# Another order of score tiles, value products and transposes in the first batch of a fused attention, gated-FFN and token-mixing kernel

## The chip, the cores and the metric

The kernel runs on one core of a Trainium2 chip. The time is that of the device for one execution, in microseconds (us); lower is better. The engines are named as the profile names them: PE (TensorE, with PEld for its weight loads), DVE (VectorE), ACT (ScalarE), POOL (GpSimd) and SP (SyncE, which here issues every DMA; SPq in the trace).

## What is computed

Three stages follow each other, in float32, for 4 batches of 576 tokens. Causal attention with 8 heads of 64 channels has a decay bias that comes from a running sum of `s`. A gated FFN (512 to 1024 channels) mixes its gate over the tokens. A last stage mixes tokens with two 576x576 matrices. Cut to what matters:

```python
scores = scale * q @ k.T + min(-(cum_i - cum_j), 0)      # cum = cumsum(relu(s)), causal mask
attn = softmax(scores); x = concat_heads(attn @ v)       # [4, 576, 512]
h = gelu(x @ w_in); u, v = h[..., :512], h[..., 512:]
x2 = x + (u * (w_sg @ layernorm(v) * g_ln + b_sg)) @ w_out
theta = x2 @ w_theta
y = w_tok_r @ (x2 * cos(theta)) + w_tok_i @ (x2 * sin(theta))
out = (x2 + y) + relu((x2 + y) @ w_ch)
```

## The kernel before

**Precision.** Products are made of halves: each operand is rounded (`rnd`, L82 on ACT, L86 on POOL) and its rest is kept (`sub`, L90), so that most products are three matmuls. The FFN's weights arrive as 64-bit words and are converted by `split64`: an ACT scaling of the raw words (L465, `wtab<-wraw`), three DVE integer operations (L466, L467, L469), an ACT rounding (`wih`, L82) and a POOL rest (`wil`, L90). The weights `w_sg` come through `gt` into `wsh` and `wsl`.

**Heads.** `attention` runs through the 32 heads. For head g it draws on three generators. `score_units(g)` has six units: four score tiles `sc` of 128, 192, 320 and 448 columns, and one wide tile `sc2` (2 x 288 columns) in two units. Each tile gets a row maximum on DVE (L292) and an exponential on ACT (L293), which writes `E`. `transpose_units(g - 1)` transposes the `E` of the head in front on PE (L332) and copies the results to `Ef` and `E0`. It also sends the reciprocal row sums through `R`, `rT` and the DRAM buffer `rd`. After every second head `pv_units` makes the value product `Y` of a pair of heads, and a small remainder `Z` that is written into a corner of the wide score tile then in use. DVE multiplies both with the factors `xT`, loaded back from `rd` (L390 for `Z`, L391 for `Y`). `split_head(g + 2)` and `load_head(g + 4)` prepare later heads: a POOL rounding of `qA`, POOL rests for `qA` and `kB`, and loads of `Q` and `K`.

**Buffers.** The four `sc` tiles, `R`, `Y` and (from the second batch on) the transposes share four PSUM buffers. The wide tile has one buffer, so that the next wide tile waits for the exponential of this one and for L390, which reads `Z` out of it. In the first batch the transposes have two PSUM buffers of their own. The parts `qB` and `kB` have two buffers, one for even and one for odd heads.

**What sets the order.** `ORDER` and `ORDER_V` (L56, L57) are strings that are followed for every head: `s` draws a score unit, `t` a transpose unit, `v` a value unit, and `p` prepares later heads (and loads `xT`). After a batch of 8 heads its FFN becomes a filler: `pace` draws small pieces of it between the units of the following heads. In the first batch there is no such filler. What the code says is then sorted by a list scheduler, which simulates the engines and sets the final order of each engine's instructions; each engine works through its own list strictly in that order. A batch's first FFN products (`fo`) need the converted `w_in`, whose loads (`wraw`) are held back until the loads of head 10.

Of the kernel before, what the change touches and what calls it, by code (L numbers as in the profile page):

```python
# [18 lines left out]
B, H, S, D = 4, 8, 576, 64  # L19
# [30 lines left out]
class Kernel:  # L50
# [2 lines left out]
    LATER, LATER_W = 10, 0  # L53


    ORDER = "ssstsstspttt"  # L56
    ORDER_V = "sssvtsvstspvttt"  # L57
    RATIO_IN, RATIO_GATE, RATIO_W = 0.94, 0.66, 0.8

    def __init__(self, tc, q, k, v, s, w_in, g_ln, w_sg, b_sg, w_out, w_th, w_tr, w_ti, w_ch, out):  # L60
# [358 lines left out]
    def attention(self):  # L419
        n = B * H  # L420
        self.load_head(2)
        self.load_v(2)
        self.load_head(3)
        for g in range(n + 1):
            su = self.score_units(g) if g < n else iter(())
            tu = self.transpose_units(g - 1) if g > 0 else iter(())

            gp = g - 2 if (g - 2) % H != H - 1 else 0
            pv = self.pv_units(gp) if gp > 0 and gp % 2 else iter(())
            if g == n:  # L430
                self.wide = None
            for o in self.ORDER_V if gp > 0 and gp % 2 else self.ORDER:
                if o == "p":
                    if g > 0 and g % 2 == 0:
                        self.load_r(g // 2 - 1)
                    if g + 2 < n:
                        self.split_head(g + 2)
                    if g + 4 < n:
                        self.load_head(g + 4)
                    if g % 2 and g + 3 < n:  # L440
                        self.load_v(g + 3)
                    continue
                c = next({"s": su, "t": tu, "v": pv}[o], None)
                if c is not None:
                    self.pace(c)
            self.run_units([tu])
            if g > 0 and g % H == 0:
                self.run_units([self.pv_units(g - 1)])
                b = g // H - 1
                if b < B - 1:  # L450
                    self.drain()
                    self.fill = self.ffn(b)
# [524 lines left out]
```

## Time and profile before

| | us |
|---|---|
| median of 3 runs | 708.98 (708.6 to 710.29) |
| the profiled execution | 710.52 |
| its span, first to last instruction | 708.7 |
| what lies around the span | 1.8 |
| PE busy in the span | 662.4 (93%) |
| heads 0 to 7 up to the end of pair 3's value product | the first 76.3 |

The profile shows one execution. A row of the timeline has the start, the duration, the engine, the line and the operation; in brackets at its end stands the idle time before it and what ended that. Many PE instructions have L93, since one helper records them; the tile's name tells them apart.

### The profile page before, as it was taken

Reading aid. Unit: us, or ns where it says so; the run is one execution under the profiler, and the core shown is the slowest. Engines: PE = TensorE matmul, PEld = TensorE weight load, DVE = VectorE, ACT = ScalarE, POOL = GpSimd, SP = SyncE. Lnnn points to the kernel's source line nnn. Section 1 sums busy time; section 2 is a strip of 40 time slices with the busy share of each in tenths; the row PEclk is TensorE's granted clock in tenths of the full one; section 3 lists DMA queues with packets and bytes.
Section 4 is the critical chain, followed back from the end, with each engine's and each line's share of the span. In section 5 each row is a group of like instructions: output and inputs, shape, how many; then the busy total and the mean of one; then the engine's idle time right before and its main releaser. Section 6 shows DMA issues by size and latency. Waiting matters only on the chain.

```text
span 708.7 us, 12076 instructions
## 1 busy us (share of the span) xinstructions
PE 662.4 (93%) x4288; PEld 580.9 (82%) x4288; DVE 455.4 (64%) x902; ACT 371.7 (52%) x856; POOL 261.3 (37%) x273
## 2 busy tenths in 40 slices
PE   6899789799999999999999769998999999999998
PEld 4667557588879788897879669887999989989997
DVE  5566687766438544484449998898976368368522
ACT  3566656677367743786427534673753255156100
POOL 6556564458426554375237653423000100010000
PEclk9899989999999999999999989999999999999999
DMA  4646666624423354321143778972000300300101
GB/s 131 188 142 193 203 196 182 183 78 147 125 83 109 102 154 142 103 84 44 68 143 104 243 240 297 328 255 85 34 1 25 110 1 1 134 1 1 68 1 68
DMA packets 52972, 85.02 MB, mean 120 GB/s; under 512 B 9968, under 2 KB 19600, under 8 KB 52912
## 3 DMA queue, kind: packets, MB, share of 16 engines
q1 hardware_dynamic: 52912, 84.25, 38.3%
q8 instruction: 34, 0.56, 0.3%
q14 instruction: 26, 0.21, 0.1%
HBM read 60.38 MB, written 19.10 MB: 112 GB/s over the span
## 4 chain that ended last, share of the span: by engine, by line
PE 49%; DVE 7%; DMA 4%; ACT 3%; issue 2%; POOL 0%; SPq 0%; DVEq 0%; ACTq 0%
PE yo L93 16%; PE co L93 7%; PE fo L93 7%; PE th L93 6%; PE Y L93 3%; PE wo L93 3%; PE sc L93 3%; PE T L332 2%; DVE wta L469 1%; DVE wta L467 1%; DMA x2T<-x2d 1%; PE tp L720 1%; DVE wta L466 1%; DVE gl L90 1%; DMA wraw<-in_moe_w_ch 1%
## 5 line engine op out<-in xcount | busy, mean ns | idle before, releaser
L293 ACT ACTIVATE E<-sc,negm 128x448 f32<-128x448 f32 (+4 forms) x160 | 87.0, 551 | 51.4 <-DVE negm L292 50.3
L292 DVE TENSOR_REDUCE negm<-sc 128x1 f32<-128x448 f32 (+4 forms) x160 | 73.6, 481 | 43.4 <-PE sc L93 42.2
L93 PE MATMUL yo<-wkh,zl 128*128 128x288 f32 x288 | 85.3, 297 | 0.0
L93 PE MATMUL yo<-wkh,zh 128*128 128x288 f32 x288 | 85.2, 296 | 0.0
L93 PE MATMUL yo<-wkl,zh 128*128 128x288 f32 x288 | 85.1, 296 | 0.0
L332 PE MATMUL T<-ident,E 128*128 128x128 f32 x400 | 73.4, 298 | 5.0 <-ACT E L293 3.4
L93 PE MATMUL sc<-kA,qA 128*128 128x128 f32 (+2 forms) x192 | 64.9, 359 | 9.5 <-ACT E L293 7.8
L332 PEld LDWEIGHTS T<-ident,E 128*128 128x128 f32 x400 | 58.2, 194 | 17.2 <-issue 5.7
L93 PE MATMUL sc<-kB,qB 68*128 68x128 f32 (+3 forms) x192 | 61.6, 331 | 3.4 <-DMA qB<-cpos 1.8
L93 PE MATMUL fo<-x,wih 128*128 128x288 f32 x256 | 58.4, 306 | 1.5 <-ACT vT L607 0.8
L86 POOL TENSOR_SCALAR xt<-x2s 128x128 fp32r<-128x128 f32 x16 | 9.9, 634 | 134.2 <-DVE x2s L90 134.2
L93 PEld LDWEIGHTS yo<-wkh,zh 128*128 128x128 f32 x288 | 54.1, 188 | 0.3
L93 PEld LDWEIGHTS yo<-wkl,zh 128*128 128x128 f32 x288 | 54.1, 188 | 0.2
L93 PEld LDWEIGHTS yo<-wkh,zl 128*128 128x128 f32 x288 | 53.9, 188 | 0.2
L93 PE MATMUL co<-u,wch 128*128 128x288 f32 x256 | 53.1, 295 | 0.0
L93 PEld LDWEIGHTS sc<-kA,qA 128*128 128x128 f32 x192 | 38.6, 209 | 16.3 <-ACT E L293 8.4
L90 POOL TENSOR_TENSOR kB<-K,kA 64x576 fp32r<-64x576 f32 x32 | 46.6, 1456 | 10.5 <-ACT kA L82 9.1
L93 PE MATMUL wo<-gh,woh 128*128 128x288 f32 x128 | 40.4, 319 | 9.1 <-DVE xr L697 6.4
L86 POOL TENSOR_SCALAR qA<-Q 128x576 fp32r<-128x576 f32 x32 | 22.6, 705 | 69.7 <-PE sc L93 29.9
L90 POOL TENSOR_TENSOR qA<-Q,qA 64x576 fp32r<-64x576 f32 x32 | 46.3, 1446 | 2.6
L93 PE MATMUL Y<-Ef,vr 128*64 128x512 f32 (+3 forms) x256 | 47.0, 444 | 0.0
L93 PEld LDWEIGHTS fo<-x,wih 128*128 128x128 f32 x256 | 43.3, 192 | 3.9 <-issue 1.2
(169 smaller groups left out, 1878.5 us busy)
## 6 DMA issues: line engine op xcount, KB each, us to landing
Q<-in_q SPq DMA_DIRECT2D x64, 144.0 KB
K<-in_k SPq DMA_DIRECT2D x64, 144.0 KB
qB<-qA SPq DMA_DIRECT2D x32, 144.0 KB
xT<-rd SPq DMA_DIRECT2D x32, 144.0 KB
xd<-xT SPq DMA_DIRECT2D x16, 288.0 KB
gd<-uT SPq DMA_DIRECT2D x16, 288.0 KB
gr<-gd SPq DMA_DIRECT2D x16, 288.0 KB
xr<-xd SPq DMA_DIRECT2D x16, 288.0 KB
```

What stands on the lines that cost most here:

```text
L86: nc.gpsimd.tensor_scalar(out, src, 1.0, 1.0, op0=ALU.mult, op1=ALU.mult)
L90: e.tensor_tensor(out, a, f32(hi), op=ALU.subtract)
L93: self.nc.tensor.matmul(out, lhsT, rhs, start=start, stop=stop)
L292: nc.vector.tensor_reduce(negm[:, c:c + 1], o, axis=ax, op=ALU.max, negate=True)
L293: nc.scalar.activation(out, o, AF.Exp, bias=negm[:, c:c + 1], accum_out=sm[:, j * 5 + c:j * 5 + c + 1])
L332: nc.tensor.transpose(T[:, col:col + P], e, self.ident)
L466: nc.vector.tensor_scalar(ta.bitcast(U32), ta.bitcast(U32), 3, None, op0=ALU.logical_shift_left)
L467: nc.vector.scalar_tensor_tensor(ta.bitcast(U32), Hi, 0x80000000, ta.bitcast(U32), op0=ALU.bitwise_and, op1=ALU.bitwise_or)
L469: nc.vector.scalar_tensor_tensor(ta.bitcast(U32), L, 29, ta.bitcast(U32), op0=ALU.logical_shift_right, op1=ALU.bitwise_or)
L720: nc.tensor.transpose(tp[0:r, dt * P:(dt + 1) * P], x2T[:, dt, a:a + r], self.ident)
```

## The change

Up to and with head 8 (`g <= H`) two other strings are followed. All six score units of a head stand first, then `p`. Where a pair's value product is due, its three units come next (`ALONE_V`). The transposes of the head in front come last. A new letter `r` separates the loading of `xT` from `p`: in the later batches it stands right ahead of `p`, as before, and in the new order it stands after the second transpose unit, which writes `rd`.

```diff
-    ORDER = "ssstsstspttt"
+    ORDER = "ssstsstsrpttt"
     ORDER_V = "sssvtsvstspvttt"
+
+    ALONE, ALONE_V = "sssssspttrttt", "sssssspvvvttt"
...
-            for o in self.ORDER_V if gp > 0 and gp % 2 else self.ORDER:
-                if o == "p":
+            order = (self.ORDER, self.ORDER_V, self.ALONE, self.ALONE_V)
+            for o in order[2 * (g <= H) + (gp > 0 and gp % 2)]:
+                if o == "r":
                     if g > 0 and g % 2 == 0:
                         self.load_r(g // 2 - 1)
+                    continue
+                if o == "p":
                     if g + 2 < n:
                         self.split_head(g + 2)
```

The lines of the file move by two ahead of `attention` (L93 becomes L95). The scheduler sorts the new text anew, so that the lists of all engines differ from head 1 on, on PE until late in the attention. Three places follow. In their names a number behind a tile tells one buffer from another.

**First place: PE in the middle of the batch, around the value product of pair 2 (heads 4 and 5).** Before, between score tiles of head 7; the fences have the matmuls of this stretch in the order in which PE runs them:

```order
L93 MATMUL sc<-kA,qA 128x192
L93 MATMUL sc<-kA,qA 128x320
L332 MATMUL T<-ident,E 128x128 x3
L93 MATMUL Y<-E_75,v_79 128x512
L93 MATMUL Y<-Ef,vr 64x512 x2
L332 MATMUL T<-ident,E 128x128 x2
L93 MATMUL Y<-Ef,vr 64x384 x2
L93 MATMUL Y<-Ef,vr 64x128 x2
L93 MATMUL Y<-Ef,vr 64x256 x2
L93 MATMUL sc<-kB_74,qB_73 128x128
L93 MATMUL sc<-mask,identr 128x128
```

With the change, the same place (`sc_734` is the wide tile of head 6, `sc_815` that of head 7):

```order
L95 MATMUL sc_734<-kB_72,qB_71 128x288
L95 MATMUL sc_734<-mask,identr 128x128
L95 MATMUL sc<-kA,qA 128x448
L95 MATMUL sc<-kB_74,qB_73 128x448
L95 MATMUL sc<-mask,identr 128x128
L95 MATMUL Y<-E_75,v_79 128x512
L95 MATMUL Y<-Ef,vr 64x512 x2
L95 MATMUL Y<-Ef,vr 64x384 x2
L95 MATMUL Y<-Ef,vr 64x128 x2
L95 MATMUL Y<-Ef,vr 64x256 x2
L95 MATMUL sc_815<-kA,qA 128x288
```

The value product has moved behind all four narrow score tiles of head 7, and nothing stands between its parts any more; the head's wide tile follows it, and the wide tile of the head in front stands just ahead. The six score units do not end up in a row.

**Second place: DVE and SP where the first weights are converted.** `sc_1072` to `sc_1104` are score tiles of head 10, `sc2_1031` is the wide tile of head 9, and L390 to L391 (L392 to L393 with the change) take `Z` and `Y` of pair 3 (heads 6 and 7). DVE before:

```order
L292 TENSOR_REDUCE negm1_86<-sc_1091 128x1
L390 TENSOR_TENSOR xT_932<-sc2_913,xT_932 128x64
L391 TENSOR_TENSOR xT_932<-Y_963,xT_932 128x512
L292 TENSOR_REDUCE negm1_86<-sc_1104 128x1
L292 TENSOR_REDUCE negm0_85<-sc2_1031 128x1
L252 TENSOR_SCALAR Q2_945<-Q2_945 128x576
L312 TENSOR_SCALAR sm1_90<-sm1_90 128x10
```

DVE with the change:

```order
L294 TENSOR_REDUCE negm1_86<-sc_1104 128x1
L254 TENSOR_SCALAR Q2_924<-Q2_924 128x576
L471 TENSOR_SCALAR wtab_991<-wtab_991 128x512
L472 SCALAR_TENSOR_TENSOR wtab_991<-wraw_990,wtab_991 128x512
L474 SCALAR_TENSOR_TENSOR wtab_991<-wraw_990,wtab_991 128x512
L471 TENSOR_SCALAR wtab_991<-wtab_991 128x512
L392 TENSOR_TENSOR xT_948<-sc2_906,xT_948 128x64
L393 TENSOR_TENSOR xT_948<-Y_963,xT_948 128x512
L472 SCALAR_TENSOR_TENSOR wtab_991<-wraw_990,wtab_991 128x512
L474 SCALAR_TENSOR_TENSOR wtab_991<-wraw_990,wtab_991 128x512
L294 TENSOR_REDUCE negm0_85<-sc2_1031 128x1
```

The products with `xT` now stand behind one whole weight conversion and the first step of a second; before, they stood ahead of all conversions. The DMA queue of SP at the same place, before:

```order
L362 DMA xT_932<-rd_61 64x576 x2
L227 DMA Q2_945<-in_q 64x576 x2
L229 DMA K2_946<-in_k 64x576 x2
L402 DMA xd_57<-xT_932 128x576
L462 DMA wraw_990<-in_moe_w_in 128x1024 x2
```

SP with the change:

```order
L231 DMA K2_925<-in_k 64x576 x2
L229 DMA Q2_924<-in_q 64x576 x2
L348 DMA rd_61<-rT_945 10x128
L467 DMA wraw_990<-in_moe_w_in 128x1024 x2
L364 DMA xT_948<-rd_61 64x576 x2
```

The loads of `xT` have moved behind the first two loads of weights.

**Third place: PE behind the wide tile of head 9.** Before:

```order
L93 MATMUL sc2_1031<-mask_161,identr_154 128x128
L332 MATMUL T_1120<-ident_149,E_881 128x128 x2
L332 MATMUL T_1098<-ident_149,E_881 128x128
L93 MATMUL sc2_1117<-kA_936,qA_935 128x288
L93 MATMUL sc2_1117<-kB0_72,qB0_71 128x288
L332 MATMUL T_1120<-ident_149,E_881 128x128 x2
```

With the change:

```order
L95 MATMUL sc2_1031<-mask_161,identr_154 128x128
L95 MATMUL fo_1172<-wih_242,x_515 128x512
L95 MATMUL fo_1228<-wih_242,x_515 128x512
L95 MATMUL fo_1172<-wil_243,x_515 128x512
L95 MATMUL fo_1172<-wih_242,x_515 128x512
L95 MATMUL fo_1228<-wil_243,x_515 128x512
L95 MATMUL fo_1228<-wih_242,x_515 128x512
L95 MATMUL fo_1172<-wih_242,x_687 128x512
L95 MATMUL fo_1228<-wih_242,x_687 128x512
L334 MATMUL T_1098<-ident_149,E_881 128x128
L95 MATMUL sc2_1117<-kA_915,qA_914 128x288
```

The first eight products of the FFN stand here now, ahead of the wide tile of head 10; before, they came behind the value product of pair 4 and the wide tile of head 11. On ACT, too, the exponential of `sc2_1031` now stands behind the scaling of three `wraw` tiles, two roundings to `wih`, one of `x`, one of `K` and one of `w_sg`; before, it stood ahead of them.

## Rows read from the trace of the kernel before

**Rows 1.** The page: busy time of the engines, share of the span, instructions.

```profile
PE 662.4 (93%) x4288; PEld 580.9 (82%) x4288; DVE 455.4 (64%) x902; ACT 371.7 (52%) x856; POOL 261.3 (37%) x273
```

**Rows 2.** Windows: length, busy time by engine, granted PE clock, DMA share and rate.

```profile
27.00:76.20 49.20, 45.43 (x271) 33.18 (x271) 31.79 (x64) 31.64 (x99) 29.26 (x27) 0.93 0.58 169
76.20:98.40 22.20, 18.48 (x104) 13.65 (x103) 18.27 (x29) 12.81 (x38) 12.48 (x12) 0.92 0.70 205
98.40:108.50 10.10, 7.48 (x41) 6.74 (x40) 9.05 (x17) 6.54 (x19) 5.90 (x5) 0.83 0.68 197
108.50:150.00 41.50, 34.81 (x205) 28.90 (x206) 29.48 (x60) 28.93 (x71) 19.37 (x15) 0.96 0.58 164
240.00:300.00 60.00, 59.81 (x392) 51.09 (x392) 28.57 (x60) 34.92 (x88) 30.87 (x31) 1.00 0.44 129
```

**Rows 3.** Waits of PE from 27.4 to 76.2: total, times, longest.

```profile
PE sc L93 <- DMA qB<-qA: 1.6, 1, 1.6
PE sc L93 <- ACT E L293: 1.4, 4, 0.4
```

**Rows 4.** Timeline of PE from pair 3's value product to the first FFN products.

```profile
72.87 1.10 PE L93 MATMUL Y<-E,v 128*128 128x512 f32 x2 [0.58 <-ACT x L82]
...
75.89 0.39 PE L93 MATMUL Y<-Ef,vr 128*64 128x256 f32 x2
...
83.14 0.35 PE L93 MATMUL sc<-kA,qA 128*128 128x288 f32 x1
...
83.80 0.45 PE L332 MATMUL T<-ident,E 128*128 128x128 f32 x2
...
86.95 0.22 PE L93 MATMUL sc<-mask,identr 128*128 128x128 f32 x1
...
95.75 0.68 PE L93 MATMUL fo<-wih,x 128*128 128x512 f32 x2
...
97.43 1.14 PE L93 MATMUL fo<-wih,x 128*128 128x512 f32 x3
```

**Rows 5.** Timeline of POOL: the rest of `K` of a head, the rest of `qA`.

```profile
74.71 1.40 POOL L90 TENSOR_TENSOR kB<-K,kA 64x576 fp32r<-64x576 f32 x1
...
91.37 1.47 POOL L90 TENSOR_TENSOR qA<-Q,qA 64x576 fp32r<-64x576 f32 x1
```

**Rows 6.** Timeline of SP's queue: loads of a head, then of weights.

```profile
80.38 1.23 SPq L229 DMA_DIRECT2D K<-in_k  x2
...
83.53 0.92 SPq L462 DMA_DIRECT2D wraw<-in_moe_w_in  x2
...
97.19 0.33 SPq L462 DMA_DIRECT2D wraw<-in_moe_w_in  x1
```

**Rows 7.** Timeline of ACT: scalings of `wraw` that waited for their transfer.

```profile
90.81 0.67 ACT L465 ACTIVATE wtab<-wraw 128x512 f32<-128x512 f32 x1 [0.56 <-DMA wraw<-in_moe_w_in]
...
101.62 0.67 ACT L465 ACTIVATE wtab<-wraw 128x512 f32<-128x512 f32 x1 [0.25 <-DMA wraw<-in_moe_w_in]
```

**Rows 8.** Timeline of DVE: the product with `Z`, and steps of the first conversions.

```profile
82.29 0.21 DVE L390 TENSOR_TENSOR xT<-sc,xT 128x64 f32<-128x64 f32 x1
...
91.62 1.78 DVE L467 SCALAR_TENSOR_TENSOR wtab<-wraw,wtab 128x512 uint32<-128x512 uint32 x1
93.43 0.69 DVE L469 SCALAR_TENSOR_TENSOR wtab<-wraw,wtab 128x512 uint32<-128x512 uint32 x1
94.04 0.42 DVE L466 TENSOR_SCALAR wtab<-wtab 128x512 uint32<-128x512 uint32 x1
```

**Rows 9.** Timeline of PE: the two longest waits after 98 us.

```profile
103.46 0.33 PE L93 MATMUL sc<-kA,qA 128*128 128x128 f32 x1 [2.06 <-ACT E L293]
...
142.34 0.40 PE L93 MATMUL sc<-kA,qA 128*128 128x288 f32 x1 [4.01 <-ACT E L293]
```

**Rows 10.** Timeline of ACT: the Gelu of batch 0, and the exponential behind it.

```profile
137.14 2.34 ACT L617 ACTIVATE vT<-vT 128x2560 f32<-128x2560 f32 x1
...
141.44 0.77 ACT L293 ACTIVATE E<-sc,negm 128x576 f32<-128x576 f32 x1
```

## The prediction, made before the changed kernel ran

> **What bounds the kernel now.** I first read the page: PE is busy for 662.4 of 708.7 us [rows 1], so time can only be won where PE waits or where its clock is low. Then the windows by stage, to see where that is. From 240 to 300 us, where the FFN of one batch fills the attention of the next, PE is busy for 59.81 of 60 us at a granted clock of 1.00 [rows 2]: nothing is to be had there. In the first batch, which has no filler, it is busy for 45.43 of 49.2 us between 27 and 76.2, with a clock of 0.93; and from 76.2 to 150, where the weights are converted and the first FFN starts, for 18.48 of 22.2, 7.48 of 10.1 and 34.81 of 41.5, with 0.92, 0.83 and 0.96 [rows 2]. So the waits that an order can change lie between 27 and 150 us: 3.8 us in heads 2 to 7, and 3.7 + 2.6 + 6.7 = 13.0 us behind them. Third, the waits of PE in the heads: 1.6 us of the 3.8 are one wait for head 2's `qB` [rows 3], whose preparation the change leaves where it was. Last, the timelines of the engines around 83 us, where the lists of before and after part most. The stretch behind 76 us is late work of the first batch, so the change reaches it although its strings concern heads 0 to 8.
>
> All numbers below are differences to the profiled execution, which took 710.52 us (1.8 more than its span); the three shown runs have a median of 708.98, and I put the difference on that median.
>
> **The change, part by part.** It removes and adds no instruction; it only moves them.
>
> Heads 2 to 7. Of 3.8 us of waits 1.6 stay, so at most 2.2 can go. The value product of a pair now stands in one piece between the narrow tiles and the wide tile of a head (first place), and covers the wide exponential of the head in front. But the wide tile of the same head comes only then, and `Z` waits for its exponential, the last narrow tile of the next head for a buffer, and the next transposes for copies on ACT and DVE. I take -1.0, with -2.2 and +1.0 as bounds (a wait of 0.4 us [rows 3] more in each of the pairs).
>
> The handover to the weights. I count from the end of pair 3's `Y`, 75.89 + 0.39 = 76.28 in [rows 4]. Before, the wide tile of head 9 started at 83.14, or 6.9 us later, 0.64 us after the L390 that freed its buffer had ended (82.29 + 0.21 in [rows 8]). After the change that L390 stands on DVE behind a whole conversion and a first step of the next (second place). So it waits for the second `wraw` to land. When is that loaded? Head 8's wide tile now comes after `Y` and two small tiles, ending near 1.6 (it takes 83.80 - 83.14 = 0.66 us). Only then may POOL overwrite the even `kB`; with the rounding of `K` ahead of it that starts at 2.3. POOL's two rests of 1.40 us each (nearest row for both [rows 5]) end at 3.7 and 5.1; they free `K` and `Q` for the loads of head 12, and the second pair of these, 1.23 us as in [rows 6], and the small `rd` write stand ahead of `wraw`, which is therefore issued near 6.8. Before, it was issued at 83.53, or 7.3: no earlier in sum, and the transfer is what counts. The second `wraw` landed at 90.81 then, 7.3 us after the first issue [rows 6, 7]; so now at 14.1. Add the scaling on ACT of 0.67 [rows 7], L466's 0.42 and L390's 0.21 [rows 8]: the wide tile of head 9 starts at 15.4 instead of 6.9. The work ahead of it is done before 9, so PE stands idle for some 6 us. Since this stretch now includes head 8's wide tile (0.66), which ran earlier before, the loss is 15.4 - 6.9 - 0.7 = +7.8.
>
> Its bounds: a single `wraw` landed 101.62 - 97.19 = 4.4 us after its issue [rows 6, 7]; were that so for the second of the pair, issued half a microsecond behind the first, it would be there at 11.7, the wide tile could start at 13.0, and the loss would be +5.4. On the other side the first conversion may end later than the second scaling: its three DVE steps take 0.42 + 0.69 + 0.69 = 1.8 us at best, but one of them took 1.78 at 91.62 while POOL ran a rest from 91.37 [rows 5, 8], and with two such they take 4.0. With a first landing 0.9 ahead of the second, at 13.2, that gives 13.2 + 0.7 + 4.0 + 0.6 = 18.5 and a loss of +10.9. I take the middle value, because POOL's next work behind head 10's rests is a `wil`, which waits for that conversion itself, so DVE should have its fast times. The Trainium skill, SBUF — State Buffer, section "SBUF: two separate sides", says that DVE and GpSimd lock a shared pair of ports for a whole instruction; the trace agrees (1.78 us with POOL at work, 0.69 at 93.43 without). By that rule too the conversion would take the fast 1.8 us.
>
> From there to the wide tile of head 10. Eight FFN products and the exponential of head 9's wide tile, which ACT reaches only after two more roundings and a third scaling, now stand in between (third place). DVE needs the product with `Y`, two conversion steps and the maximum, some 3.6 us from times as in [rows 8]; ACT a scaling, a rounding and the exponential (0.77 in [rows 10]), some 2.5; the wide tile ends near 22. That is 6.6 us after 15.4. Before, it was 86.95 + 0.22 - 83.14 = 4.0 us, and the eight products took 97.43 + 1.14 - 95.75 = 2.8 us later on [rows 4]. These cancel: 0, from -0.5 to +2.
>
> What is given back. Before, PE waited 2.06 us at 103.46 for an exponential behind such a conversion, and 4.01 us at 142.34 for one behind the Gelu [rows 9]. The first is the wait that the handover now has earlier; the conversions are further ahead of the attention, so I strike it: -2.1 (0 at worst). As to the second, the Gelu takes ACT from 137.14 on for 2.34 us, and the exponential comes at 141.44 [rows 10]. After the change a pair's whole value product, 76.28 - 72.87 = 3.4 us of PE work [rows 4], and FFN products stand on PE between the last tile ahead of the Gelu and the first that needs the exponential behind it. I take -2.5, between 0 and -4.0.
>
> New waits. The lists are sorted anew as far as 380 us. Head 11's `qA` and `kB` stand on POOL behind the first `wil`, and a longer idle time brings more work at a low clock, as the 0.83 between 98.4 and 108.5 shows after waits [rows 2]. I take +1.0, from 0 to +4.
>
> Sum: -1.0 + 7.8 + 0 - 2.1 - 2.5 + 1.0 = +3.2 us. Behind 150 us PE has no free time to take this up, so it reaches the end: 708.98 + 3.2 = 712.2 us.
>
> **The rivals.** *Everything is given back* (faster). The FFN now starts with its conversions ahead of the attention, and all PE waits between 98.4 and 150 could go, as PE has either filler or a value product at hand. Windows show 2.6 + 6.7 = 9.3 us of them [rows 2]. For it speaks the Gelu's new cover; against it, that part of these waits is for copies and roundings on ACT, which no order of PE removes. With 8.5 of the 9.3 us gone, the handover at its lower +5.4 and the heads at -1.0 it gives -4.1: 704.9 us. It decides as soon as more than 8 us come back.
>
> *The transfers are quick* (no change). The second `wraw` could land in the 4.4 us of a single one, since no load of `Q` and `K` follows it directly now. Then the handover costs +5.4 and the sum is +0.8: 709.8 us. `xT`, queued behind it, would have to be as quick. The Trainium skill, SBUF — State Buffer, "The DMA setup-cost knee", has 2 us plus the bytes over 436 GB/s; for the two `wraw` of 512 KB that is an estimate of 4.4 us in sum, and with it the forecast would be this rival's. The trace differs: 7.3 us for the pair.
>
> *The hole grows* (slower). With the slow conversion (+10.9) and nothing given back at 142 us the sum is -1.0 + 10.9 + 0 - 2.1 + 0 + 1.0 = +8.8: 717.8 us. For it speaks that POOL may still be at head 10's rests when DVE starts.
>
> *The strings do little*: the scheduler undoes them in part, as the first place shows (wide tiles slip behind narrow ones of the next head). Were the handover's list the only real difference, we would still be at the forecast; so this has no time of its own.
>
> **How the numbers follow.** A measurement of this kernel can tell about 0.3%, or 2.1 us, from no change. Forecast, +1 to +6: 0.45, of which 0.10 lies within 2.1 us. Everything given back: 0.20, all faster. Quick transfers: 0.15, all within. The hole grows: 0.15, all slower. The rest, 0.05, I spread as 0.03 slower, 0.01, 0.01. So slower 0.35 + 0.15 + 0.03 = 0.53, same 0.10 + 0.15 + 0.01 = 0.26, faster 0.21. The range reaches from just above the first rival, 705.5 (which leaves 0.1 below), to just above the third, 718.0; the likeliest case alone has 710.0 to 715.0.
>
> **What would show it.** In the changed profile: an idle time of PE of 4 us or more ahead of a wide score tile between 83 and 95 us, ended by DVE's product of `xT` with `Z`, which itself follows L471; a scaling of `wraw` on ACT that waits for its transfer just before; no PE wait above 2 us at the Gelu near 140 us. Heads 2 to 7 should end at most 2 us sooner. I am wrong if the wide tile of head 9 starts within 9 us of the end of pair 3's `Y`, or if PE's idle time between 98 and 150 us falls by more than 8 us, or grows.

## The result, and the profile after

The changed kernel takes 714.28 us (median of 19 runs, 708.86 to 720.91), the kernel before 708.98 on the same chip (19 runs). The ratio, which leaves out the one slow run of 720.91, is 1.008, interval 1.0062 to 1.0099: about 5.7 us slower (the medians differ by 5.3). The median is 2.1 above the 712.2 us forecast and inside its range. The two profiled executions differ by less, 712.44 against 710.52 us, since the first profile of before lay above its median and this one below; so terms are read from stretches of the traces, and sums from the medians.

The windows of after, as in [rows 2] (length, then busy time with instructions for PE, PE's weight loads, DVE, ACT and POOL, then granted clock, DMA share and rate):

```profile
27.00:76.20 49.20, 43.97 (x268) 31.52 (x267) 30.05 (x64) 30.03 (x96) 26.77 (x25) 0.93 0.60 172
76.20:98.40 22.20, 13.70 (x67) 10.78 (x66) 13.78 (x22) 13.40 (x34) 10.51 (x8) 0.77 0.67 192
98.40:108.50 10.10, 6.37 (x27) 5.24 (x29) 10.10 (x17) 4.49 (x14) 7.49 (x6) 0.66 0.50 149
108.50:150.00 41.50, 39.06 (x237) 31.31 (x236) 32.90 (x66) 31.03 (x74) 23.53 (x20) 1.00 0.60 173
```

PE idles 5.2 + 8.5 + 3.7 + 2.4 = 19.9 us from 27 to 150, against 16.8 before [rows 2]. And it is slower while it works: 0.77 and 0.66 of full clock where before had 0.92 and 0.83. The stage behind 108.5 is better than before, the one ahead of 76.2 worse. The timeline of PE, from the end of the first batch (start, duration, engine, line, operation, count, and in brackets the idle time ahead with what ended it):

```profile
66.00 0.45 PE L95 MATMUL sc<-kA,qA 128*128 128x448 f32 x1
...
66.55 0.69 PE L334 MATMUL T<-ident,E 128*128 128x128 f32 x4
67.08 0.27 PE L345 MATMUL R<-ident,r 128*128 128x128 f32 x1
67.59 0.61 PE L334 MATMUL T<-ident,E 128*128 128x128 f32 x3 [0.25 <-ACT Ef L338]
69.57 0.66 PE L334 MATMUL T<-ident,E 128*128 128x128 f32 x4 [1.36 <-DVE Ef L341]
71.01 1.20 PE L95 MATMUL Y<-E,v 128*128 128x512 f32 x2 [0.78 <-DVE E L357]
72.14 3.94 PE L95 MATMUL Y<-Ef,vr 128*64 128x512 f32 x16
...
83.85 0.51 PE L334 MATMUL T<-ident,E 128*128 128x128 f32 x2
91.25 0.61 PE L95 MATMUL sc<-kA,qA 128*128 128x288 f32 x1 [6.89 <-DVE xT L392]
...
97.87 0.22 PE L95 MATMUL sc<-mask,identr 128*128 128x128 f32 x1
102.13 0.47 PE L345 MATMUL R<-ident,r 128*128 128x128 f32 x1 [4.04 <-DVE r L315]
```

Pair 3's `Y` ends at 76.08 and the wide tile of head 9 starts at 91.25, 15.2 us later, where before had 6.9 [rows 4] and the forecast had 15.4. The wide tile of head 10 ends at 98.09, 22.0 after `Y` (forecast: near 22). A second hole of 4.04 us stands ahead of `R`. The timelines of DVE, SP's queue and ACT there:

```profile
88.58 0.43 DVE L471 TENSOR_SCALAR wtab<-wtab 128x512 uint32<-128x512 uint32 x1 [3.53 <-ACT wtab L470]
89.04 0.69 DVE L472 SCALAR_TENSOR_TENSOR wtab<-wraw,wtab 128x512 uint32<-128x512 uint32 x1
...
90.64 0.43 DVE L471 TENSOR_SCALAR wtab<-wtab 128x512 uint32<-128x512 uint32 x1 [0.18 <-ACT wtab L470]
90.98 0.22 DVE L392 TENSOR_TENSOR xT<-sc,xT 128x64 f32<-128x64 f32 x1
...
91.71 1.37 DVE L472 SCALAR_TENSOR_TENSOR wtab<-wraw,wtab 128x512 uint32<-128x512 uint32 x1
...
98.59 1.75 DVE L472 SCALAR_TENSOR_TENSOR wtab<-wraw,wtab 128x512 uint32<-128x512 uint32 x1
...
101.88 0.20 DVE L315 RECIPROCAL r<-sm 128x10 f32<-128x10 f32 x1
```

```profile
82.81 0.84 SPq L467 DMA_DIRECT2D wraw<-in_moe_w_in  x2
84.51 1.10 SPq L364 DMA_DIRECT2D xT<-rd  x2
```

```profile
87.88 0.66 ACT L470 ACTIVATE wtab<-wraw 128x512 f32<-128x512 f32 x1 [2.51 <-DMA wraw<-in_moe_w_in]
89.93 0.68 ACT L470 ACTIVATE wtab<-wraw 128x512 f32<-128x512 f32 x1 [1.39 <-DMA wraw<-in_moe_w_in]
```

The picture is the forecast one: `wraw` issued 6.7 us after the end of `Y` (82.81, forecast 6.8), its second half waited for until 13.9 us after it (89.93, forecast 14.1), and the product with `Z` on DVE right behind L471. The reciprocal `r`, for which `R` waits, stands on DVE behind a slow conversion step (1.75 us at 98.59), the rests `wsl` on either side of it and another step; I had given new waits 1.0 us in all. Behind 104 us PE's longest wait up to 150 is 1.09 us: the 4.01 us behind the Gelu [rows 9] are gone.

### The profile page after: what moved, and what is told of

The parts are those of the page before. It is cut to its first block, busy times and chain, and to the rows that moved or that the text cites. A ratio compares the mean times of both kernels' runs of the same rounds, so it can differ in the third digit from the quotient of the medians.

```text
span 710.7 us, 12078 instructions
## 1 busy us (share of the span) xinstructions
PE 662.4 (93%) x4288; PEld 582.1 (82%) x4288; DVE 450.3 (63%) x902; ACT 372.1 (52%) x856; POOL 263.4 (37%) x273
## 4 chain that ended last, share of the span: by engine, by line
PE 48%; DVE 7%; DMA 4%; ACT 2%; issue 2%; POOL 0%; SPq 0%; DVEq 0%; ACTq 0%
PE yo L95 16%; PE co L95 7%; PE fo L95 7%; PE th L95 5%; PE wo L95 4%; PE Y L95 3%; PE sc L95 3%; PE T L334 2%; DMA xr<-xd 1%; DVE wta L472 1%; DVE wta L474 1%; DVE gl L92 1%; DMA wraw<-in_moe_w_out 1%; PE tp L725 1%; DVE wta L471 1%
## 5 line engine op out<-in xcount | busy, mean ns | idle before, releaser
L95 PE MATMUL yo<-wkh,zl 128*128 128x288 f32 x288 | 85.3, 297 | 0.0
L95 PE MATMUL yo<-wkh,zh 128*128 128x288 f32 x288 | 85.2, 296 | 0.0
L95 PE MATMUL yo<-wkl,zh 128*128 128x288 f32 x288 | 85.1, 296 | 0.0
L334 PE MATMUL T<-ident,E 128*128 128x128 f32 x400 | 71.2, 295 | 5.7 <-ACT Ef L338 2.2
L95 PE MATMUL sc<-kA,qA 128*128 128x128 f32 (+3 forms) x192 | 65.0, 358 | 10.1 <-DVE xT L392 6.9
L95 PE MATMUL sc<-kB,qB 68*128 68x128 f32 (+4 forms) x192 | 61.2, 330 | 4.1 <-DMA qB<-cpos 1.9
L95 PE MATMUL fo<-x,wih 128*128 128x288 f32 x256 | 57.1, 302 | 0.1
L95 PEld LDWEIGHTS yo<-wkh,zh 128*128 128x128 f32 x288 | 54.1, 188 | 0.3
L95 PEld LDWEIGHTS yo<-wkl,zh 128*128 128x128 f32 x288 | 54.0, 188 | 0.2
L95 PEld LDWEIGHTS yo<-wkh,zl 128*128 128x128 f32 x288 | 53.9, 188 | 0.2
L95 PE MATMUL co<-u,wch 128*128 128x288 f32 x256 | 53.1, 295 | 0.0
L95 PEld LDWEIGHTS sc<-kA,qA 128*128 128x128 f32 x192 | 38.4, 207 | 17.2 <-DVE xT L392 7.1
L95 PE MATMUL Y<-Ef,vr 128*64 128x512 f32 (+3 forms) x256 | 49.0, 457 | 0.0
L95 PE MATMUL wo<-gh,woh 128*128 128x288 f32 x128 | 39.8, 313 | 6.6 <-DVE xr L702 6.6
L95 PE MATMUL th<-wth,x2s 128*128 128x512 f32 x128 | 43.1, 402 | 2.3 <-DVE x2s L92 1.2
```

Of the source, the lines that this page charges most:

```text
L95: self.nc.tensor.matmul(out, lhsT, rhs, start=start, stop=stop)
L334: nc.tensor.transpose(T[:, col:col + P], e, self.ident)
```

## The experiments

Every run is compared with the kernel before on its own chip (medians 707.97 to 708.78).

| run | edit | median us | ratio to before, interval |
|---|---|---|---|
| the change | | 714.28 | 1.008, 1.0062 to 1.0099 |
| e1_vector_pin | conversion on DVE behind `xT`'s products | 714.12 | 1.0072, 1.0047 to 1.0097 |
| e2_vector_and_sp_pin | and `wraw` behind `xT` on SP | 714.1 | 1.0092, 1.0069 to 1.0115 |
| e3_new_order_to_head_6 | new strings for heads 0 to 6 | 710.39 | 1.0041, 1.0015 to 1.0068 |
| e4_new_order_heads_7_8 | new strings for heads 7, 8 | 709.9 | 1.0025, 1.0001 to 1.0049 |
| z_after | the change, pair 3's `Z` elsewhere | 710.89 | 1.0028, 1.0002 to 1.0053 |
| z_before | before, pair 3's `Z` elsewhere | 713.81 | 1.0066, 1.0041 to 1.009 |
| z_heads_7_8 | as e4, pair 3's `Z` elsewhere | 706.32 | 0.9964, 0.9942 to 0.9985 |
| kw_after | products nobody reads, in the hole | 730.3 | 1.0298, 1.0263 to 1.0333 |

The theory at the start was the prediction's: the loss is the handover, because DVE's list puts `xT`'s products behind a conversion. The rivals: heads 2 to 7 lose it themselves; the transfers set it, whatever DVE's list.

**DVE's list, then SP's.** In `split64`'s call, with `mul[7]` the product of pair 3's `xT` with `Y` and `xload[3]` its load (the second only in the second run):

```diff
+with self.tc.issue_after(self.mul[7].ins), self.tc.issue_after(self.xload[3].ins):
     self.split64(...)
```

> Edit: the kernel after, with the Vector engine's part of the first weight conversion held behind pair 3's two xT products; the transfers on SP stay in the order of after. Handover theory (the loss is the hole ahead of head 9's wide tile, since xT x Z stands behind a conversion that waits for its wraw transfers, and the wait of R behind more conversion steps): xT of pair 3 is loaded at 84.5 us in after and should land about 2 us later, so the wide tile starts 10 to 11.5 us after the end of pair 3's Y instead of 15.2 and the time falls by 3 to 5 us, to 709 to 711 us. Theory that heads 2 to 7 lose it: 713 to 715 us, as in after. Theory that the transfers alone set it, wherever the Vector engine's steps stand: the wide tile stays 14 to 16 us behind Y's end and the time 713 to 715 us.

> Edit: as the run with the Vector engine's pin, and the conversion's wraw transfers are held behind pair 3's xT load on SP as well. Handover theory: xT is issued near 82.8 us, the wide tile starts 7 to 10 us after Y's end (6.9 in before), and the time is 707.5 to 710 us; the conversion is 1 to 2 us later, which the wait of 4.0 us at R or the first product with wih may show. Theory that heads 2 to 7 lose it: 713 to 715 us. Theory that the order of the transfers is what costs: this run alone gains, the Vector engine's pin by itself nothing.

Neither gained. With the list turned round, DVE's product with `Z` came 15.0 us behind the end of pair 3's `Y`, where the change has 14.9, and PE's hole was 7.02 us:

```profile
89.66 0.22 DVE L393 TENSOR_TENSOR xT<-sc,xT 128x64 f32<-128x64 f32 x1 [6.12 <-ACT wtab L471]
```

The row names ACT's scaling (88.89 + 0.66 = 89.55) as what ended the wait, but with the pin no step of a conversion stands ahead of the product. `xT`'s transfer, issued at 83.07 behind both `wraw`, is the other candidate. The traces also record when a transfer lands, and `xT` landed at 89.54 here. In the change it was issued at 84.51 and landed at 90.79, 0.2 us ahead of the product at 90.98. The run z_after below, with the same order of transfers, names it in its row: there DVE stood 0.73 us idle for `xT` itself.

```profile
88.42 0.69 DVE L474 SCALAR_TENSOR_TENSOR wtab<-wraw,wtab 128x512 uint32<-128x512 uint32 x1
89.84 0.23 DVE L394 TENSOR_TENSOR xT<-Z,xT 128x64 f32<-128x64 f32 x1 [0.73 <-DMA xT<-rd]
```

```profile
82.11 0.84 SPq L469 DMA_DIRECT2D wraw<-in_moe_w_in  x2
83.90 1.10 SPq L364 DMA_DIRECT2D xT<-rd  x2
```

So `xT` takes 5.9 to 6.5 us from its issue in these three traces when it follows two `wraw`; in the change DVE's list held the product only 0.2 us longer than that. With `xT` ahead of `wraw` on SP (second run) it was waited for too, but its product started 3.6 us after its issue at 86.06:

```profile
89.62 0.23 DVE L393 TENSOR_TENSOR xT<-sc,xT 128x64 f32<-128x64 f32 x1 [3.17 <-DMA xT<-rd]
```

There the holes shrank to 4.1 and 2.2 us, yet the median did not move. `xT` was issued later than expected (86.06 for 82.8), so that the wide tile still started 12.4 us behind `Y`, not 7 to 10; and behind 98 us PE had new waits of 2.0, 1.9 and 1.6 us for exponentials and copies. The first form of the theory (DVE's list alone) falls. For the first run the answer that the transfers set the hole came true (15.3 us, 714.12 us), but its time is also that of the heads' theory; that the second run alone would gain did not. The wide tile's wait as such, and heads 2 to 7, remain to be tested.

**Which heads.** The condition `g <= H` becomes `g < H - 1`, then `H - 1 <= g <= H`:

> Edit: the new strings for heads 0 to 6 alone; heads 7 and 8 keep the old ones, so that on the Vector engine pair 3's xT products stand ahead of the first conversion as in before. Handover theory: the hole is not there, nor what the new strings gave back at the Gelu; 707 to 710.5 us, that is within 2 us of before. Theory that heads 2 to 7 lose it: 712 to 715 us.

> Edit: the new strings for heads 7 and 8 alone; heads 0 to 6 keep the old ones. On the Vector engine pair 3's xT products then stand behind the first conversion as in after. Handover theory: the wide tile of head 9 starts 13 to 16 us after pair 3's Y and the time is 712.5 to 716 us, as in after. Theory that heads 2 to 7 lose it: 707 to 710 us.

The two medians answer in opposite ways: 710.39 lies at the edge of what the handover theory expected (707 to 710.5), 709.9 within what the heads' theory expected (707 to 710). So neither theory holds alone. Both parts lose, +2.9 us (1.1 to 4.8) with heads 0 to 6 alone, +1.8 (0.1 to 3.5) with heads 7 and 8 alone, together nearly the 5.7 of the change. The second is the smaller, though its hole is whole (6.29 us ahead of the wide tile, then 4.04 ahead of `R`). Where do heads 0 to 6 lose? Windows of PE alone (length, busy time, clock, DMA share, rate) at the end of the batch. First before, then e3:

```profile
66.00:72.00 6.00, 4.85 (x33) 1.00 0.66 192
72.00:78.00 6.00, 5.38 (x34) 1.00 0.71 205
```

```profile
66.00:72.00 6.00, 3.87 (x18) 0.76 0.53 160
72.00:78.00 6.00, 6.00 (x28) 0.67 0.42 132
```

Then after, e4 and z_heads_7_8:

```profile
66.00:72.00 6.00, 3.60 (x19) 0.99 0.58 164
72.00:78.00 6.00, 6.00 (x33) 0.72 0.48 151
```

```profile
66.00:72.00 6.00, 5.54 (x32) 1.00 0.69 203
72.00:78.00 6.00, 5.10 (x35) 1.00 0.52 153
```

```profile
66.00:72.00 6.00, 5.91 (x36) 1.00 0.68 199
72.00:78.00 6.00, 5.74 (x42) 1.00 0.47 151
```

With the new strings up to head 6, all six traces have PE busy for 3.60 to 3.96 of the 6 us from 66 to 72, and in five of them the clock then stands at 0.50 to 0.87 between 72 and 78, that is partly or wholly at 1.2 GHz; with the old strings up to head 6, all five traces have 4.67 to 5.91 us and a clock of 1.00. The timeline of after above shows what differs: `R`, seven transposes and `Y` of pair 3 are alone on PE from 67.08, each group waiting for a copy of the one ahead (0.25, 1.36, 0.78 us), because the scores that used to stand between them have been run already. With the old strings (z_heads_7_8) they are still there:

```profile
67.08 0.99 PE L334 MATMUL T<-ident,E 128*128 128x128 f32 x7
67.93 0.47 PE L95 MATMUL sc<-kA,qA 128*128 128x448 f32 x1
...
68.51 0.28 PE L345 MATMUL R<-ident,r 128*128 128x128 f32 x1
68.71 0.43 PE L95 MATMUL Z<-E,v 128*128 128x64 f32 x2
69.24 1.12 PE L95 MATMUL Y<-E,v 128*128 128x512 f32 x2
```

The low clock has its price in a row. In e1_vector_pin, whose PE list is that of after up to 84 us, the clock stayed full, and the sixteen products of pair 3's `Y` took 2.37 us where after needed 3.94; they ended at 74.63, for 76.08 in after:

```profile
72.26 2.37 PE L96 MATMUL Y<-Ef,vr 128*64 128x512 f32 x16
```

One pair of traces says how much it is in all. From 82.2 us on (78.5 in e4) the PE lists of after and e4 are the same, and from 112 to 380 us after runs 3.2 us behind throughout. So what heads 0 to 6 lose there lies ahead of 82 us, and no new order of PE behind it can be the cause. At head 8's last narrow tile (66.00 in after, 67.04 in e4) after is still 1.0 us ahead; at the end of pair 3's `Y` (76.08, and 72.93 in e4) it is 3.2 behind. The rows of e4, where head 8's wide tile stands in the gap between the two parts of `Y`:

```profile
67.04 0.47 PE L95 MATMUL sc<-kA,qA 128*128 128x448 f32 x1
...
69.40 1.94 PE L95 MATMUL Y<-Ef,vr 128*64 128x512 f32 x10
...
72.07 0.86 PE L95 MATMUL Y<-Ef,vr 128*64 128x128 f32 x6
```

With e1 between them at 74.63, about half of the 3.2 us goes with the low clock (an estimate from three executions); the rest, and the lead of 1.0, went in the chain of copies. The ratios agree in sign and size: from e4 to the change these heads cost 3.9 us (1.0025 to 1.008), and 2.9 from before to e3.

**Heads 0 to 7 by themselves, and before once more.** The programs of the next three runs end after pair 3 (`n = H`, the `x` tiles written to the output); the fourth is the kernel before.

> Left out: everything behind batch 0's attention (heads 8 to 31, the feed-forward part, the mixing); the program ends after pair 3's product and writes its x tiles to the output. Strings of before. With the run of the same cut program with the new strings it measures the term of heads 2 to 7 by itself, with no weight conversion and no handover. In before pair 3's products stand at 82.4 us; some 85 to 110 us in all with the program's start and the writes. The difference new minus old is what counts: see the run with the new strings.

> Left out as in the cut program with the old strings; the new strings for all heads. Theory of the prediction (heads 2 to 7 gain about 1 us): 0 to 2 us shorter than the cut program with the old strings. Theory from the run with the new order to head 6 (which came out 2.9 us slower than before): heads 2 to 7 lose, 1.5 to 4 us longer than with the old strings. Theory that the strings as such cost nothing and that run's loss was a re-sorting behind head 8: within 0.5 us.

> Left out as in the cut program with the old strings; the new string only for heads without a pair's value product in them (0, 1, 2, 4, 6, 8), the old one for heads 3, 5 and 7. If the loss of the new strings comes from a head's transposes standing in one row behind its six score units, most of the difference between the two cut programs is here (over two thirds); if it comes from moving the pair's value product ahead of the transposes, less than one third.

> The kernel before, unchanged, for a second profile of it. The profiled execution of before shown ahead took 710.52 us, 2 us above the median of its runs. If that is a matter of the clock that was granted between 27 and 50 us (0.86), the second profile has a clock of 0.93 or more there and pair 2's products stand 1 to 2.5 us earlier than 70.6 us; if it is spread over the whole span, pair 2's products stand within 0.5 us of 70.6.

Medians of 83.1, 79.69 and 83.67 us, of six runs each that spread over 3.7 to 4.7 us: the new strings gain 3.4 us here, and the new string for heads without a value product gains nothing by itself. It contradicts e3 only at first sight. Of the 3.4 us PE has 1.9, since its `Y` of pair 3 ended at 69.79 instead of 71.73. The rest is `xT`, which with the old strings is issued behind writes of the output (at 69.31, for 65.97 with the new ones), so that DVE waited for it:

```profile
73.27 0.23 DVE L392 TENSOR_TENSOR xT<-sc,xT 128x64 f32<-128x64 f32 x1 [5.02 <-DMA xT<-rd]
```

Further, the cut program has the new string at head 7 too, which e3 has not, and in the whole program the strings of heads 7 and 8 do bring this point forward: `Y` of pair 3 ends at 72.93 in e4, where the two profiles of before have 76.28 and 75.17. And nothing follows in it that a low clock could slow down: with the new strings the clock is 1.00 from 66 to 72 us and 0.60 from 72 to 78, where PE has no product left. In the whole program head 8 follows, whose scores the old order uses as filler. A part cut out of its surroundings measured another question. The second profile of before took 709.77 us; it has a clock of 0.93 from 27 to 50 us, and pair 2's products at 69.49 instead of 70.6, as expected; the ends of the later pairs' `Y` stay 1.1 to 1.3 us earlier up to the last pair. That much of any comparison with the first profile goes with the clock ahead of 50 us.

**The wide tile's wait taken away.** `Z` of pair 3 goes to a bank of the `fo` tag, which nothing needs at that time, so head 9's wide tile no longer waits for `xT`; in the change, in before, and in e4:

```diff
     Z = wide[:, 0, 320:384]
+    if g == H - 1:
+        Z = self.psF.tile([P, 512], F32, name="Z", tag="fo")[:, 0:64]
```

> Edit: the kernel after, with pair 3's Z in a bank of the 'fo' tag instead of the free columns of the wide bank; head 9's wide tile then waits neither for the xT x Z product nor for anything that stands behind the weight conversion on the Vector engine, wherever that conversion stands. Handover theory in its new form (it is the wait of the wide tile, and the half clock that follows the hole, that lose the time; heads 2 to 7 by themselves gain about 3 us, as the cut programs showed): no PE idle over 3 us between 76 and 100 us, granted clock 0.9 or more there (0.77 and 0.66 in after), and 704 to 710 us. Theory that the loss lies in heads 2 to 7: 713 to 715 us, as in after. Theory that the loss is only deferred work which comes back as other waits: 711 to 715 us with the hole elsewhere.

> Edit: the kernel before, with pair 3's Z in a bank of the 'fo' tag, as the control of the run z_after. If heads 2 to 7 gain with the new strings once the handover is out of the way, as in the cut programs, this one is 1 to 4 us slower than z_after. If the new strings lose in heads 2 to 7, it is 1 to 4 us faster than z_after. By itself the edit should be worth little here, since in before the xT x Z product stands ahead of the conversion: 705 to 709 us.

> Edit: pair 3's Z in a bank of the 'fo' tag as in z_after, but the new strings for heads 7 and 8 alone; it differs from z_after in heads 0 to 6 only, so it measures their term once more with no hole behind it. Theory from the cut programs (heads 2 to 7 gain about 3 us with the new strings): 1.5 to 4 us slower than z_after's ratio of 1.0028 gives, a ratio of 1.005 to 1.0085. Theory from the run with the new order to head 6 (they lose about 2.9 us in the whole program, where a sparse stretch of PE near 66 to 72 us is followed by a half clock): a ratio of 0.996 to 1.0005, full clock between 66 and 78 us, and the best version of all. Theory that heads 0 to 6 are worth nothing either way: 1.001 to 1.0045.

In z_after no wait over 2.02 us is left between 76 and 100, the clock is 0.85 and 0.96 in the second and third window of [rows 2], and it is 3.7 us faster than the change (1.008 to 1.0028; the expected 704 to 710 just missed). In e4, which has the same hole, the edit gains 4.3 (z_heads_7_8, 1.0025 to 0.9964). That is what the wide tile's wait seems to cost in sum, but the edit also sorts the lists anew, so its size is not shown by itself. z_after is still not faster than before. Its own timeline shows what came back, first PE, then ACT:

```profile
141.63 0.42 PE L95 MATMUL sc<-kA,qA 128*128 128x288 f32 x1 [3.78 <-ACT E L295]
```

```profile
136.18 2.34 ACT L624 ACTIVATE vT<-vT 128x2560 f32<-128x2560 f32 x1
...
139.43 1.28 ACT L295 ACT_TABLE_LOAD   x1
140.73 0.77 ACT L295 ACTIVATE E<-sc,negm 128x576 f32<-128x576 f32 x1
```

The exponential behind the Gelu is 4.5 us after the Gelu's start, and whether PE has work for that time is decided by how the lists happen to fall: PE waited 4.0, 4.0, 3.9, 4.6 and 3.8 us there in before (twice), e3, z_before and z_after, and at most 0.9 in after, e4 and z_heads_7_8. z_before lost 4.7 us, where 705 to 709 was expected, by an edit that took no work and added none; its longest waits behind 98 us are this one (4.6) and one of 2.4 us for `Y`. That it is 2.7 us slower than z_after was to mean that heads 2 to 7 gain. Its trace does not bear that out: against the second profile of before it is 0.6 us behind at the end of pair 3's `Y` and 6.7 at that of the third pair after it, so that it lost behind these heads. Which of its new lists' differences makes up the sum stays open.

z_heads_7_8 has neither the sparse end of the batch nor the hole nor the wait behind the Gelu, and is the only version faster than before: 706.32 us (ratio 0.9964, 0.9942 to 0.9985). It differs from z_after by 4.5 us, as the theory that heads 0 to 6 lose had expected; up to 2.9 of these can be the Gelu's wait, so this pair does not size these heads again.

**PE kept at work in the hole.** 80 products of 128 x 128 into free columns of head 8's wide bank, ahead of head 9's wide tile, and the first FFN product held behind that tile:

```diff
+if g == H + 1:
+    for _ in range(80):
+        self.mm(self.wide[:, 1, 320:448], self.identr, self.mask, True, True)
```

> Edit: the kernel after, with 80 products of 128 x 128 that nobody reads (mask by identity, into free columns of the wide bank) ahead of head 9's wide tile, in the stretch where PE stands idle, and the first product of the feed-forward held behind that tile. Nothing waits less; PE is only busy in the hole. Theory that the hole itself is what is lost: 713 to 717 us, no gain. Theory that half of the loss is the half clock that PE gets after the hole: the granted clock between 88 and 98 us is 0.9 or more instead of 0.5 to 0.55, and the time is 709 to 712 us.

It tested something else, and neither of the expected times came. The products waited for `xT` like the wide tile whose bank they share, and then ran at half clock ahead of everything:

```profile
94.21 17.33 PE L95 MATMUL sc<-mask,identr 128*128 128x128 f32 x80 [7.18 <-DVE xT L397]
```

These 17.3 us made the program 16 us longer than the change, with the clock at 0.50 from 94 to 114 us. It shows only that PE has little slack behind the hole; how much of the loss is the hole and how much the clock after it was not separated.

## Why the prediction was right, and where it was not

- *Direction and size*: slower, 714.28 for 712.2, and the hole is the forecast one. But the first term stayed inside its bounds for a reason that the prediction did not have; so far it was luck.
- *Heads 2 to 7, -1.0 (from -2.2 to +1.0)*: counted as the prediction does, up to the end of pair 3's `Y`, they ended 0.2 sooner than in the first profile of before and 0.9 later than in the second (76.08, for 76.28 and 75.17), inside the bounds. Two larger effects hide in it. The new strings of heads 7 and 8 bring this end 2.2 to 3.3 us forward (72.93 in e4), and those of heads 0 to 6 take 3.2 of that back. I had summed the waits that could go, and not asked what would be left for PE once the scores were done: transposes, `R` and `Y` of the last pair in a chain of copies, and a low clock behind it. The run with heads 0 to 6 alone (+2.9) shows the loss in the sum.
- *The handover, +7.8*: the hole was right to 0.2 us (15.2 for 15.4). The forecast path, by the second `wraw`, its scaling and L471, did end last, at 90.98; but `xT` landed only 0.2 us earlier, so that a pin on DVE had no more than that to gain. I had mentioned `xT`'s place behind `wraw` and not priced it.
- *Stretch to head 10's wide tile, 0*: right, 22.0 for 22.
- *Given back, -2.1 and -2.5*: the wait behind the Gelu went from 4.01 to under 0.7, more than taken; e4 shows it gone too, with an order of the other heads as before. The 2.06 us at 103 did not go: there is the wait of 4.04 for `R` instead.
- *New waits, +1.0 (0 to +4)*: low. `R` alone costs 2.0 more than the wait that stood there, and the clock of 0.77 and 0.66 comes on top.
- *All terms behind `Y`* were put at 7.8 - 2.1 - 2.5 + 1.0 = +4.2. In the traces after loses 2.6 to 2.8 us between the end of pair 3's `Y` and that of the last pair, and e4 2.5 to 2.7. The 5.7 of the medians is more than these executions hold up to there (2.4 to 3.7); the profiled ones lie 1.8 us below the median of after and 1.0 to 1.5 above those of before, which can be the rest.
- *The rivals*: quick transfers did not come: the second scaling started 7.1 us after the issue of the pair, as before (7.3). The hole stayed at the middle of its bounds, since the first conversion had its fast steps (0.43 + 0.69 + 0.69) while POOL stood idle, up to 91.25; the L472 at 91.71, beside POOL's `wil`, took 1.37. The Trainium skill, SBUF — State Buffer, section "SBUF: two separate sides", has a DVE instruction with two SBUF inputs and a GpSimd one that reads SBUF lock a shared pair of ports against each other for a whole instruction; the trace agrees again (1.37 us beside POOL, 0.69 without). Everything given back needed 8 us between 98 and 150; PE's idle time there fell from 9.3 to 6.2.

## What to carry to other kernels

Before moving work forward, look at what it leaves behind: filler that is run early is missing where the chain of copies is, and the price is the wait plus the low clock that follows. A tile that borrows free columns of a bank ties two schedules together; giving the borrowed piece its own bank took away a hole that pins on the engine and on the queue did not, though where there was no hole the same edit lost 4.7 us. And test a part inside the whole program: cut out, the strings of heads 0 to 7 gained 3.4 us; in place, those of heads 0 to 6 lost 2.9.

## What the runs showed of the hardware

With the same instructions in both, a stretch partly or wholly at 1.2 GHz between 72 and 78 us went with the order of heads 0 to 6: in five traces of six with the new one, in none of five with the old. With one and the same order of PE, the same sixteen products took 2.37 us at full clock and 3.94 in the trace with the low one. Two loads of 144 KB took 5.9 to 6.5 us behind two of 512 KB on the same queue, and 3.6 us ahead of them. Executions of before spread over 8.8 us, those of the change over 6.8 and one 5.2 beyond, and the two profiles first compared showed 1.9 us of a difference of 5.7.
